# Placing the block sums of a channel MLP, and moving two column copies from VectorE to GpSimd

## The chip, the cores and the metric

The kernel runs on one core of a Trainium2 chip. The metric is the device time of one execution in microseconds (us), from the launch to the end on that core. Three executions of the kernel before took 618.13, 616.25 and 618.18 us; their median is 618.13 us. Inputs and the output are float32 in HBM; inside the chip the operands of the matrix products are fp16 and their sums are float32 in PSUM.

## What is computed

The input is x with 8 batches of 3008 positions and 256 features. First the real part of a two-dimensional Fourier transform over positions and features is taken, and then an MLP mixer block is applied to it: a token MLP across the positions and a channel MLP across the features, each with a residual add.

```python
X = np.fft.fft(np.fft.fft(x, axis=1), axis=2).real           # (8, 3008, 256)
h = np.maximum(X.transpose(0, 2, 1) @ w_tok1, 0) @ w_tok2     # 3008 -> 256 -> 3008
u = X + h.transpose(0, 2, 1)
h2 = np.maximum(u @ w_ch1, 0) @ w_ch2                         # 256 -> 1536 -> 256
return (u + h2).astype(np.float32)
```

## The kernel before

**Stages.** For each batch b, a generator `front(b)` (lines 436 to 567) makes the transform and the token MLP and yields after each small piece: products in PSUM tiles `pz`, `pw`, `pt1`, `pq`, `py`, `pu`, with a VectorE (DVE) or ScalarE (ACT) instruction behind each. Its result is u, laid out with features on the partitions, in six tiles `ut` of 512 positions (the last has 448). Another generator, `fold(b)` (line 414), prepares the input of a batch with fp16 adds on DVE, from SBUF to SBUF. The channel MLP takes one `ut` tile at a time. There are 6 tiles in each of 8 batches, so 48 blocks.

**The two halves of a block.** `mm1` (line 584) makes the hidden layer: 12 groups of 128 hidden features, each two TensorE (PE) products of 128x512 and a ReLU on ACT into the tile `c1` (called c in the profile). `mm2` (line 673) makes the output from `c1`, adds the residual u, and stores it. 42 of the 48 blocks use `mm2_sums` (line 620), a two-by-two block scheme that needs seven block products in place of eight; the other six are called `plain` (line 581) and multiply directly. The scheme needs sums of quarters of `c1`, which DVE makes in `block_sums` (line 599). Four instructions are made for the lower three groups of each half of `c1` (`slice(0, 3)`, called "lower" below) and four for the upper three (`slice(3, HC)`, "upper"):

- number 0: sb0 = a21 + a22
- number 1: sb1 = sb0 - a11
- number 2: a21 = a11 - a21, written over a21 in `c1`
- number 3: sb2 = a12 - sb1

**The order of work.** It is written out by hand; each engine takes its instructions in program order. A block has four steps s = 0 to 3, and `sub = 4 * c + s` counts the 24 steps of a batch. In each step PE gets three of the 12 groups of `mm1` for the current block, then `mm2` step s for the block before (`prev`), with pieces of the front work around it: `own` are the last pieces of this batch's front, `nxt` those of the next batch's, half of them before `mm2` and half after. `plan` and `own_plan` say how many pieces each step takes, and `fold` pieces come at the end of a step from sub 10 (15 in the first batch). In this text "step 1" means s = 1.

**What each step of mm2_sums reads.** Step 0: `c1` directly. Step 1: sb0, then sb1. Step 2: the new a21. Step 3: a22, then sb2. The PSUM tiles are px and py (`pa` and `pb` in the code). The second product of step 1 goes to the part of px that the first product of step 0 used, and waits until DVE has read px in step 0 (line 645, `osb<-px,m` in the profile). The DVE reads in step 3 are `osb<-px,rt` and `osb<-py,m`.

**The residual.** `turn_u` (line 571) transposes `ut` by DMA from SyncE's queue into `rt`, four buffers in turn. `edges` (line 611) copies one or two columns within `rt` (two instructions for c of 3 to 5, otherwise one; 72 in all), so that one slice can be read backwards. A part of the residual is added on GpSimd (POOL): 128x256 float32 in step 0 (line 646) and 128x512 in step 3 (line 660), SBUF to SBUF, 42 of each. POOL's queue also issues the loads of x (`load_x`, line 122).

**Where the sums stand.** In the kernel before: upper 0 and 1 in step 0 behind `mm1`; upper 2 and 3 in step 1 behind `mm1`; lower 0 and 1 in step 2 behind `mm2`; lower 2 and 3 in step 3 behind `mm2`.

Of the kernel before, what the change touches and what calls it, by code (L numbers as in the profile page):

```python
# [40 lines left out]
def kernel(  # L41
# [9 lines left out]
    nc = tc.nc  # L51
# [70 lines left out]
    def load_x(b, between=(None, None)):  # L122
        xp = xin.tile([KR, NR, D], FP16, tag="xp", name="xp")
        xm = xin.tile([KG, NR - 1, D], FP16, tag="xm", name="xm")
        for i in range(2):
            for q, n in ((0, 32), (32, NQ - 32)):
                p0 = i * NQ + q
                nc.gpsimd.dma_start(
                    out=xp[p0:p0 + n, :, :],
                    in_=dram(x_t, (b * S + 16 * i + 64 * q) * D,  # L130
                             [[64 * D, n], [1, NR * D]]))
        xmf = xm[:].rearrange("p t d -> p (t d)")
        for k in range(2):
            if between[k] is not None:
                between[k]()
            gather(xmf[:, 8 * D * k:8 * D * (k + 1)], x8, ix8[0:KG, b, k:k + 1])
        return xp, xm
# [23 lines left out]
    for t in (tp, tq):  # L161
        for i in range(2):
            h = slice(64 * i, 64 * i + 64)
            nc.scalar.activation(
                out=t[h, :, 64 - 64 * i:128 - 64 * i],
                in_=pcol[h, :].unsqueeze(2).to_broadcast([64, NG, 64]),
                func=AFT.Copy, scale=0.0)
    nc.scalar.activation(out=w1m[64:128, NG - 1, :],
                         in_=pcol[64:128, :].to_broadcast([64, DTOK]),
# [52 lines left out]
    HC = NCT // 2  # L222
    wst = const.tile([P, 4, HC, P], FP16, tag="wst")

    def weight_sums():
        b11, b12, b21, b22 = (wc2[:, HC * j:HC * j + HC, P * k:P * k + P]
                              for j in range(2) for k in range(2))
        for o, x, y, op in ((0, b12, b11, AT.subtract), (2, b22, b12, AT.subtract),
                            (1, wst[:, 2], b11, AT.add), (3, b21, wst[:, 1], AT.subtract)):
            nc.vector.tensor_tensor(out=wst[:, o], in0=x, in1=y, op=op)  # L230

    def swap_wc1(h):
        nc.sync.dma_start(out=wc1[1][:, h, :], in_=wc1[0][:, h, :])
        nc.sync.dma_start(out=wc1[1][0:1, h, :], in_=wc1[0][0:1, 1 - h, :])
# [172 lines left out]
    def align_w2(j):  # L407
        th, k = j // 4, slice(16 * (j % 4), 16 * (j % 4) + 16)
        copy(0, w2p[:, th, k, 0:NQ], w2v[:, th, k, :])
# [4 lines left out]
    def fold(b, engs):  # L414
        xp, xm = x_tiles.pop(b)
        eo = perb.tile([KR, NR, D], FP16, tag="eo", name="eo")
        state[b] = {"eo": eo}
        add, sub = AT.add, AT.subtract
        for s, (t0, t1) in enumerate(((13, 17), (9, 13), (5, 9), (1, 5))):
            tt = engs[s].tensor_tensor  # L420
            t = slice(t0, t1)
            rv = slice(16 - t0, 16 - t1 if t1 < 17 else None, -1)
            tt(out=xp[:, t, 1:D], in0=xp[:, t, 1:D], in1=xm[0:KR, rv, D - 1:0:-1], op=add)
            yield
            if t0 == 1:
                tt(out=xp[:, 1:NR, 0], in0=xp[:, 1:NR, 0], in1=xm[0:KR, ::-1, 0], op=add)
                tt(out=eo[:, :, 0], in0=xp[:, :, 0], in1=xp[:, :, 0], op=add)
                t = slice(0, t1)
            tt(out=eo[:, t, 1:129], in0=xp[:, t, 1:129], in1=xp[:, t, 255:127:-1], op=add)
            yield  # L430
            tt(out=eo[:, t, 129:256], in0=xp[:, t, 1:128], in1=xp[:, t, 255:128:-1],
               op=sub)
            yield
# [137 lines left out]
    def turn_u(b, c):  # L571

        rt = work.tile([P, 4, D + 16], FP16, tag="rt", name="rt", bufs=4)
        for h in range(2):
            nc.sync.dma_start_transpose(
                out=rt[:, :, h * P:(h + 1) * P], in_=state[b]["ut"][c][:, h, :])
        return rt
# [3 lines left out]
    def plain(b, c):  # L581
        return (b, c) == (0, 0) or c + 1 == NCH and (b % 2 == 0 or b + 1 == BB)

    def mm1(b, c, c1, cts):
        ut = state[b]["ut"][c]
        n = min(CW, S - CW * c)
        wc = wc1[c >= 3]
        for i in cts:
            ct = CTS[i]
            pc = ps_mm("pc")  # L590
            for h in range(2):
                nc.tensor.matmul(pc[:, 0:n], lhsT=wc[:, h, ct * P:(ct + 1) * P],  # L592
                                 rhs=ut[:, h, 0:n], start=(h == 0), stop=(h == 1))
            if i % 3 < 2 or (b, c) != (0, 0):
                nc.scalar.activation(out=c1[:, ct, 0:n], in_=pc[:, 0:n], func=AFT.Relu)  # L595
            else:
                ts(c1[:, ct, 0:n], pc[:, 0:n], 0.0, AT.max)

    def block_sums(c1, sb, k, which):
        hi = slice(HC + k.start, HC + k.stop)  # L600
        a11, a21 = c1[:, k, 0:D], c1[:, k, D:CW]
        a12, a22 = c1[:, hi, 0:D], c1[:, hi, D:CW]
        sums = ((sb[:, 0, k], a21, a22, AT.add),
                (sb[:, 1, k], sb[:, 0, k], a11, AT.subtract),
                (a21, a11, a21, AT.subtract),
                (sb[:, 2, k], a12, sb[:, 1, k], AT.subtract))
        for i in which:
            o, x, y, op = sums[i]
            nc.vector.tensor_tensor(out=o, in0=x, in1=y, op=op)  # L609

    def edges(rt, c):
        for o, i in ((D, 0), (0, P)) if c >= 3 else ((D, P),):
            nc.vector.tensor_copy(out=rt[:, :, o:o + 1], in_=rt[:, :, i:i + 1])

    lower, upper, turned_ = slice(0, P), slice(P, D), slice(D, P, -1)

# [100 lines left out]
    def pair(b, c1):  # L717

        if b % 2 == 0 and b + 1 < BB:
            state["ch"] = work.tile([P, NCT, 64], FP16, tag="ch", name="ch")  # L720
            nc.vector.tensor_copy(out=state["ch"][:], in_=c1[:, :, CW - 128:CW - 64])
        elif b % 2:
            nc.vector.tensor_copy(out=c1[:, :, CW - 64:CW], in_=state["ch"][:])


    def take(g, n):
        for _ in range(n):
            next(g, None)
# [41 lines left out]
    prev = None  # L770
    turned_u = {(0, 0): turn_u(0, 0)}
    for b in range(BB):
        nxt = front(b + 1) if b + 1 < BB else iter(())
        folds = fold(b + 2, [nc.vector] * 4) if b + 2 < BB else None
        for c in range(NCH):
            c1 = work.tile([P, NCT, CW], FP16, tag="c1", name="c1", bufs=2)
            box = {"rt": turned_u.pop((b, c))}
            if not plain(b, c):
                box["sb"] = work.tile([P, 3, HC, D], FP16, tag="sb", name="sb", bufs=2)
            if c + 1 == NCH and b % 2:  # L780
                pair(b, c1)
            for s in range(4):
                sub = 4 * c + s
                n = plan[b > 0][sub]
                mm1(b, c, c1, range(3 * s, 3 * s + 3))
                if s < 2 and prev is not None and not plain(*prev[0:2]):
                    block_sums(prev[2], pbox["sb"], slice(3, HC), (2 * s, 2 * s + 1))
                take(own, own_plan[b > 0][sub])
                take(nxt, n // 2)
                if prev is not None:  # L790
                    mm2(*prev, s, pbox)
                if s >= 2 and not plain(b, c):
                    block_sums(c1, box["sb"], slice(0, 3), (2 * s - 4, 2 * s - 3))
                if b == 0 and sub < 16 and sub % 2:
                    align_w2(sub // 2)
                take(nxt, n - n // 2)
                if s == 2 and c + 1 < NCH:
                    turned_u[b, c + 1] = turn_u(b, c + 1)
                if s == 3 and c + 1 == NCH and b + 1 < BB:
                    turned_u[b + 1, 0] = turn_u(b + 1, 0)  # L800
                if b == 0 and sub == 4:
                    weight_sums()
                if b == 0 and sub == 3:
                    for h in range(2):
                        swap_wc1(h)
                if b == 0 and 3 <= sub < 9:
                    take(early, 2)
                    if sub == 8:
                        x_tiles[2] = load_x(2)
                if folds is not None and sub >= fold_at[b > 0]:  # L810
                    take(folds, 1 + (b == 0))
                    if sub == fold_at[b > 0] + (5 if b == 0 else 11) and b + 3 < BB:
                        x_tiles[b + 3] = load_x(b + 3)
            if c + 1 == NCH and b % 2 == 0:
                pair(b, c1)
            prev, pbox = (b, c, c1), box
        own = nxt
# [32 lines left out]
```

## Time and profile before

| what | value |
|---|---|
| median of the three executions | 618.13 us |
| the profiled execution, own time | 616.26 us |
| its span, first to last instruction | 614.2 us |
| outside the span (the difference) | 2.1 us |
| granted TensorE clock | 1.000 |
| ACT busy | 442.0 us (72%) |
| POOL busy | 139.3 us (23%) |
| `edges` on DVE (L613) | 72 instructions, 13.3 us, mean 184 ns |
| POOL add in step 0, 128x256 | 42, mean 758 ns |
| POOL add in step 3, 128x512 | 42, mean 1437 ns |

The profile is of one execution, and every duration in this text is from it. A group line gives the line of the kernel, engine and operation, output and inputs by the program's names, shapes and a count, then the busy time of the group in us, the mean of one instruction in ns, and the idle time of the engine just before them. A row of the timeline gives the start and the length in us; rows of one kind that follow one another are merged ("x24"), and in brackets stands the idle time before the row and what ended it. PE products overlap in these records, so the row of a later product can begin before the row of an earlier one ends.

### The profile page before, as it was taken

The numbers are of one execution on the slowest core, as the hardware profiler recorded it, in microseconds if no ns is written. First come the engines' busy times: TensorE is split into PE (matmuls) and PEld (weight loads), VectorE is DVE, ScalarE is ACT, GpSimd is POOL, SyncE is SP. The second block draws the span as 40 slices with busy tenths as digits, with TensorE's granted clock in tenths as the row PEclk, the third lists the DMA queues.
The fourth block names the chain that finished last, engine by engine and source line by source line (L and its number), as shares of the span: only waits on it lengthen the run. The fifth ranks groups of instructions, "written<-read, shape, count | busy, mean of one in ns | idle before, by whom it ended". The sixth has DMA issues, their size and how long they took to land.

```text
span 614.2 us, 15694 instructions
## 1 busy us (share of the span) xinstructions
PE 589.1 (96%) x6322; PEld 422.5 (69%) x6322; DVE 492.8 (80%) x1086; ACT 442.0 (72%) x996; POOL 139.3 (23%) x163
## 2 busy tenths in 40 slices
PE   2899999999999999999999999999999999999996
PEld 1766767667776767767676777766776767766675
DVE  8768879668998699768988789857899778867684
ACT  8866986677767777686766767777777777667772
POOL 8500413111142121302114221311121212101121
PEclk9999999999999999999999999999999999999999
DMA  8994842725347323672419234392222433232433
GB/s 137 210 192 93 183 67 56 162 57 84 53 89 141 85 52 68 118 120 52 97 44 174 53 83 74 61 183 61 53 62 58 91 53 75 65 69 60 88 62 94
DMA packets 86600, 56.52 MB, mean 92 GB/s; under 512 B 54864, under 2 KB 83472, under 8 KB 85776
## 3 DMA queue, kind: packets, MB, share of 16 engines
q1 hardware_dynamic: 78048, 37.84, 30.9%
q0 software_dynamic: 8256, 17.49, 16.5%
q8 instruction: 49, 0.80, 0.5%
q10 hardware_dynamic: 224, 0.20, 0.1%
q14 instruction: 23, 0.19, 0.1%
HBM read 34.98 MB, written 24.64 MB: 97 GB/s over the span
## 4 chain that ended last, share of the span: by engine, by line
PE 80%; DVE 8%; ACT 6%; issue 3%; POOL 1%; DMA 1%; DVEq 0%; POOLq 0%
PE pc L592 33%; PE px L633 20%; PE py L633 7%; PE pu L552 6%; PE po L690 4%; PE pt L488 3%; ACT c L595 3%; DVE sb L609 2%; DVE osb L618 2%; PE pz L445 1%; PE pw L472 1%; PE pw L473 1%; DVE ut L560 1%; PE py L519 1%; DVE yt L526 1%
## 5 line engine op out<-in xcount | busy, mean ns | idle before, releaser
L595 ACT ACTIVATE c<-pc 128x512 f16<-128x512 f32 (+1 forms) x572 | 295.8, 594 | 39.2 <-PE pc L592 19.8
L618 POOL TENSOR_TENSOR osb<-osb,rt 128x256 f32<-128x256 f32 x84 | 92.2, 1097 | 438.5 <-DVE osb L618 411.4
L592 PE MATMUL pc<-ut,wc1p 128*128 128x512 f16 x576 | 140.3, 379 | 0.0
L592 PE MATMUL pc<-ut,wc1m 128*128 128x512 f16 (+1 forms) x576 | 134.9, 370 | 0.0
L633 PEld LDWEIGHTS <-c 128*128 128x128 f16 x2016 | 121.3, 98 | 19.4 <-issue 0.3
L633 PEld LDWEIGHTS <-sb 128*128 128x128 f16 x1512 | 90.2, 98 | 14.1 <-issue 5.0
L638 ACT ACTIVATE m<-px 128x256 f32<-128x256 f32 x126 | 48.6, 386 | 69.9 <-PE px L633 45.2
L592 PEld LDWEIGHTS <-wc1p 128*128 128x128 f16 x576 | 52.2, 98 | 49.0 <-issue 2.3
L560 DVE TENSOR_TENSOR ut<-pu,yt 128x512 f16<-128x512 f32 (+1 forms) x96 | 64.1, 669 | 26.1 <-PE pu L552 26.1
L592 PEld LDWEIGHTS <-wc1m 128*128 128x128 f16 x576 | 53.0, 98 | 46.3
L609 DVE TENSOR_TENSOR sb<-c,sb 128x768 f16<-128x768 f16 x84 | 84.4, 1004 | 0.0
L633 PE MATMUL px<-wst,c 128*128 128x128 f16 x1008 | 70.0, 219 | 0.0
L633 PE MATMUL px<-wc,c 128*128 128x128 f16 x1008 | 63.1, 219 | 0.0
L618 DVE TENSOR_TENSOR osb<-py,m 128x256 f32<-128x256 f32 x84 | 35.4, 422 | 29.4 <-ACT m L638 23.2
L290 ACT ACTIVATE z<-pz 128x480 f16<-128x480 f32 (+1 forms) x60 | 40.1, 672 | 19.4 <-PE pz L445 12.4
L552 PE MATMUL pu<-w2p,uu 128*128 128x512 f16 (+1 forms) x168 | 50.0, 379 | 0.0
L609 DVE TENSOR_TENSOR c<-c 128x768 f16<-128x768 f16 x84 | 49.5, 590 | 0.0
L609 DVE TENSOR_TENSOR sb<-sb,c 128x768 f16<-128x768 f16 x84 | 46.9, 558 | 2.9
L609 DVE TENSOR_TENSOR sb<-c 128x768 f16<-128x768 f16 x84 | 45.9, 547 | 2.4 <-ACT c L595 2.4
L475 DVE SCALAR_TENSOR_TENSOR w<-alt,pw 128x131 f16<-128x131 f16 x96 | 33.0, 350 | 14.4 <-ACT w L290 14.3
L633 PE MATMUL px<-wst,sb 128*128 128x128 f16 x504 | 34.9, 219 | 3.2 <-DVE osb L618 2.6
L526 DVE TENSOR_TENSOR yt<-py,qs 128x512 f16<-128x512 f32 x48 | 30.8, 683 | 8.8 <-ACT qs L522 8.8
(163 smaller groups left out, 674.3 us busy)
## 6 DMA issues: line engine op xcount, KB each, us to landing
out_dram<-osb SPq DMA_DIRECT2D x83, 256.0 KB, 3.7
xp<-in_x_dram POOLq DMA_DIRECT2D x16, 272.0 KB
out_dram<-osb SPq DMA_DIRECT2D x11, 192.0 KB, 3.2
xp<-in_x_dram POOLq DMA_DIRECT2D x16, 127.5 KB
rt<-ut SPq DMA_TRANSPOSE x96, 3.4
w2s<-in_moe_w_tok_dram POOLq DMA_DIRECT2D x1, 1504.0 KB
w1p<-in_moe_w_tok_dram POOLq DMA_DIRECT2D x2, 384.0 KB
wc<-in_moe_w_ch_dram POOLq DMA_DIRECT2D x1, 768.0 KB
```

The source lines that it names most:

```text
L290: nc.scalar.activation(out=out_, in_=in_, func=AFT.Copy)
L475: nc.vector.scalar_tensor_tensor(out=w[:, g, 0:131], in0=alt[:], scalar=pw[:, 131:132], in1=pw[:, 0:131], op0=AT.mult, op1=AT.add)
L526: nc.vector.tensor_tensor(out=yt[:, h, CW * c:CW * c + CW], in0=py[:], in1=qs[:], op=op)
L552: nc.tensor.matmul(pu[:, 0:n], lhsT=uu[:, th, int(minus), h, :], rhs=w2_cols(b, c)[:, th], start=(th == 0), stop=(th == 1))
L560: nc.vector.tensor_tensor(out=ut[:, h, 0:n].rearrange("p (a b) -> p a b", b=64), in0=pu[:, 0:n].rearrange("p (b a) -> p a b", b=64), in1=y ...
L592: nc.tensor.matmul(pc[:, 0:n], lhsT=wc[:, h, ct * P:(ct + 1) * P], rhs=ut[:, h, 0:n], start=(h == 0), stop=(h == 1))
L595: nc.scalar.activation(out=c1[:, ct, 0:n], in_=pc[:, 0:n], func=AFT.Relu)
L609: nc.vector.tensor_tensor(out=o, in0=x, in1=y, op=op)
L618: eng.tensor_tensor(out=o, in0=x, in1=y, op=AT.add)
L633: nc.tensor.matmul(o[:, t], lhsT=a(k)[:, f:f + P], rhs=w(k), start=(first and t == 0 and k == 0), stop=(k == HC - 1), skip_group_check=True)
L638: nc.scalar.activation(out=m[:, i], in_=pa[:, 0], func=AFT.Copy)
L690: nc.tensor.matmul(po[0:n, o:o + D], lhsT=c1[:, ct, ks * P:ks * P + n], rhs=wc2[:, ct, :], start=(ct == 0), stop=(ct == NCT - 1))
```

## The change

Two edits. `edges` issues its copies on GpSimd in place of DVE. And three of the four places of `block_sums` change: upper 0 and 1 go behind the first front pieces of step 0, just ahead of `mm2`; upper 2 and 3 go to the end of step 1, behind `mm2` and all front pieces of the step; lower 2 and 3 go in front of everything in step 3 but `mm1`. Lower 0 and 1 stay where they were. Nothing is computed that was not computed before, and the instructions of PE, ACT and SyncE keep their order.

```diff
     def edges(rt, c):
         for o, i in ((D, 0), (0, P)) if c >= 3 else ((D, P),):
-            nc.vector.tensor_copy(out=rt[:, :, o:o + 1], in_=rt[:, :, i:i + 1])
+            nc.gpsimd.tensor_copy(out=rt[:, :, o:o + 1], in_=rt[:, :, i:i + 1])
...
                 mm1(b, c, c1, range(3 * s, 3 * s + 3))
-                if s < 2 and prev is not None and not plain(*prev[0:2]):
-                    block_sums(prev[2], pbox["sb"], slice(3, HC), (2 * s, 2 * s + 1))
+                def now():
+                    which = 2 * (s % 2), 2 * (s % 2) + 1
+                    if s >= 2 and not plain(b, c):
+                        block_sums(c1, box["sb"], slice(0, 3), which)
+                    elif s < 2 and prev is not None and not plain(*prev[0:2]):
+                        block_sums(prev[2], pbox["sb"], slice(3, HC), which)
+
+                if s == 3:
+                    now()
                 take(own, own_plan[b > 0][sub])
                 take(nxt, n // 2)
+                if s == 0:
+                    now()
                 if prev is not None:
                     mm2(*prev, s, pbox)
-                if s >= 2 and not plain(b, c):
-                    block_sums(c1, box["sb"], slice(0, 3), (2 * s - 4, 2 * s - 3))
+                if s == 2:
+                    now()
                 if b == 0 and sub < 16 and sub % 2:
                     align_w2(sub // 2)
                 take(nxt, n - n // 2)
+                if s == 1:
+                    now()
```

## The prediction

> **What bounds the kernel now.** I read the page first (engine totals and the DVE groups), then the waits, then the timeline of two places where TensorE is late.
>
> ```profile
> PE 589.1 (96%) x6322; PEld 422.5 (69%) x6322; DVE 492.8 (80%) x1086; ACT 442.0 (72%) x996; POOL 139.3 (23%) x163
> L609 DVE TENSOR_TENSOR sb<-c,sb 128x768 f16<-128x768 f16 x84 | 84.4, 1004 | 0.0
> L609 DVE TENSOR_TENSOR c<-c 128x768 f16<-128x768 f16 x84 | 49.5, 590 | 0.0
> L609 DVE TENSOR_TENSOR sb<-c 128x768 f16<-128x768 f16 x84 | 45.9, 547 | 2.4 <-ACT c L595 2.4
> ```
>
> The four sums have one shape; sum 3 (`sb<-c,sb`) costs 1004 ns where sum 0 costs 547. But PE carries the time, so what matters is where PE waits:
>
> ```profile
> PE px L633 <- DVE osb L618: 2.6, 8, 0.8
> PE pz L445 <- DVE ut L560: 1.6, 3, 0.7
> ```
>
> These understate the waits, since product records overlap. The chain of waits has 24 of the px products in 1.34 us, so 12 take 0.67. Counting from start to start in this way over the whole trace I get, after 40 us, 11.5 us of PE waits: 5.6 at the second product of step 1 (15 places, waiting for `osb<-px,m`), 2.1 at `pz`, 1.9 at the token products (1.3 of it in the first batch), the rest small. That is the most that any order of DVE can give back.
>
> Place A, which recurs in five batches:
>
> ```profile
> 300.06 0.42 DVE L618 TENSOR_TENSOR osb<-py,m 128x256 f32<-128x256 f32 x1
> ...
> 300.40 0.55 DVE L609 TENSOR_TENSOR c<-c 128x768 f16<-128x768 f16 x1
> 300.56 1.41 POOL L618 TENSOR_TENSOR osb<-osb,rt 128x512 f32<-128x512 f32 x1 [5.92 <-DVE osb L618]
> ...
> 300.87 1.52 DVE L609 TENSOR_TENSOR sb<-c,sb 128x768 f16<-128x768 f16 x1
> ...
> 302.58 0.41 DVE L431 TENSOR_TENSOR eo<-xp 94x508 f16<-94x508 f16 x1
> ...
> 304.13 0.83 PE L633 MATMUL py<-wst,sb 128*128 128x128 f16 x12
> 304.23 0.38 DVE L613 COPY rt<-rt 128x4 f16<-128x4 f16 x2
> 304.61 0.42 DVE L618 TENSOR_TENSOR osb<-px,m 128x256 f32<-128x256 f32 x1
> ...
> 305.09 0.83 PE L633 MATMUL px<-wst,sb 128*128 128x128 f16 x12
> ```
>
> Sum 3 starts inside POOL's add and ends 0.42 us after it (301.97, 302.39): it stood still. px could start at 304.13 + 0.67 = 304.80 and starts at 305.09, so 0.29 us are lost.
>
> Place C, at three of the changes of batch:
>
> ```profile
> 326.14 0.41 DVE L618 TENSOR_TENSOR osb<-px,rt 128x256 f32<-128x256 f32 x1
> 326.47 0.41 DVE L618 TENSOR_TENSOR osb<-py,m 128x256 f32<-128x256 f32 x1
> ...
> 327.28 2.04 DVE L609 TENSOR_TENSOR sb<-c,sb 128x768 f16<-128x768 f16 x1
> ...
> 327.72 1.18 POOL L618 TENSOR_TENSOR osb<-osb,rt 128x512 f32<-128x512 f32 x1
> 327.76 1.50 PE L633 MATMUL px<-wc,c 128*128 128x128 f16 x24
> ...
> 329.25 0.68 DVE L560 TENSOR_TENSOR ut<-pu,yt 128x512 f16<-128x512 f32 x1
> ...
> 329.98 0.37 PE L445 MATMUL pz<-t1n,eo 94*128 94x96 f16 x5 [0.72 <-DVE ut L560]
> ```
>
> The blocked sum makes L560 late, and pz waits for its PSUM buffer: 327.76 + 1.34 = 329.10, so 0.88 us. Later in the same block px (332.95) waits a further 0.37.
>
> **What the Trainium skill says.** "SBUF — State Buffer", section "SBUF: two separate sides": GpSimd shares a port pair with those DVE instructions that read two SBUF inputs or run in a two-port mode; it is an exclusive lock for a whole instruction, and the loser blocks. The trace agrees: 52 of the 84 sums 3 overlap a POOL add, and these average 1287 ns against 546 for those that don't; L475, with a PSUM input, takes 351 in both cases. "Perfetto Trace Analysis", "Identifying the Most-Contended Engine", warns that matmul busy share misjudges headroom; hence my count from starts. "GPSIMD Engine Reference", "Performance pitfalls for Q7 kernels", gives about 2.9 cycles an element for reads with steps over 8 bytes: for 4 elements next to nothing, so the fixed cost of a POOL instruction decides.
>
> **The change part by part.** I replay the measured rows in the new order, PE's natural times kept, ends overlapping by 0.08 us as in the trace. DVE loses 52 x (1287 - 546) = 38.5 us of standing in sum 3 and 13.3 us of edges; part of the standing comes back wherever the next SBUF instruction follows POOL's add.
>
> 1. *Lower 2 and 3, now ahead of the reads in step 3.* The reads come up to 0.95 us later where DVE is busy. Cover: the next px product has 1.2 to 3.0 us in hand behind `osb<-px,rt` in the stretches with fold work, and keeps at least 0.25. Cost 0; without cover up to 0.3 us a block.
>    - C: `osb<-px,rt` ends at 327.49, before PE needs it at 327.76; `osb<-py,m` at 327.83; L560, which reads PSUM, runs beside POOL's add, 327.75 to 328.43; pz waits no more. L526 waits for ACT (328.76), upper sums to 331.15, `osb<-px,m` to 331.49, before px's natural 332.95 - 0.37 - 0.88 = 331.70. Gain 1.25, 1.25 and 0.72 us at the three changes (the third pz wait is 0.35): **-3.2**.
>    - A: POOL's add moves to 301.5 to 302.9. What collides now is the fold L431, which ends at about 303.35; L475; upper 0 and 1 from 303.54 to 304.68; `osb<-px,m` ends at 305.02. Before: 305.03. Nothing gained, the collision has changed its victim.
> 2. *Upper 0 and 1 behind the first pieces of step 0.* In the blocks before the odd changes of batch (such as 174.87, waiting 0.37) L526, held by ACT until 171.89, now stands ahead of them, and `osb<-px,m` ends at 174.62 in place of 174.82: gain 0.2. Three such, two even ones with 0.1, and half of an unexplained 0.35 us of DVE standing at 318.5: **-1.0**. The last summed block, with no front work (px at 599.26, waiting 0.36): the copy L723 collides in place of sum 3, and edges are gone, so `osb<-px,m` ends 0.3 earlier: **-0.3**. Blocks such as 293.48, with 0.47 us in hand, lose: there before, POOL had waited for `c<-c` and sum 3 slipped through; now L429 collides until 292.40, then a tail copy and L560 come ahead of the sums, and `osb<-px,m` ends at 294.45, px wanted 294.36: 0.14 each in five blocks.
> 3. *Upper 2 and 3 at the end of step 1.* They now stand behind that step's last piece. At 284.62 L475 waits for ACT; the new a21 would be ready at 285.45, while px (285.25) wants its fourth weight at about 285.36: 0.14 with the release, in six blocks: **+0.7**. In A the same gives 0.08, in five blocks: **+0.4**. Queued behind are sum 3, the fold piece and `osb<-py,m`, all with room.
> 4. *Edges on POOL.* Behind them in POOL's queue are the step-0 adds and x loads, in front the step-3 add; nothing there is late (POOL is 23% busy). The plain blocks' DVE reads wait for them, more than a step later. Their price on POOL is not shown: the nearest rows are 128x1 operations of 92 (memset) to 636 ns; I take 0.2 each. On DVE they free 0.17 or 0.38 us in step 0, counted above. But POOL runs them as soon as its step-3 add ends, just where DVE's sums stand, so each can hold DVE once: between 0 and 0.4 us. I take half of it where DVE is late: 0.12 in five A and five D blocks: **+1.2**, with D's 0.14 x 5: **+0.7**.
> 5. *First batch.* The replay from 80 to 98 us moves a 0.99 us wait by -0.26 and adds about 0.5 at the new a21; the 1.28 us wait at 97.39 stays within 0.1, as DVE is the limit until there. **0 +- 1**.
>
> Sum: -3.2 - 1.0 - 0.3 + 0.7 + 0.4 + 1.2 + 0.7 = **-1.5 us**. Against the profiled execution 616.26 that is 614.8; the median of the three runs is 1.87 above that execution, and on it the forecast is 618.13 - 1.5 = 616.6.
>
> **The rivals.**
> - *Much of the wait goes* (R1). If edges cost DVE nothing and folds collide less than replayed, A, D and the first batch gain too: 4.5 + 1.5 (A) + 1 (first batch) - 0.7 = 6.3, so 611.8. For it: 52 us of DVE time leave. Against: in A and D the same POOL add meets the next fold.
> - *The collision only moves* (R2). C's gain is eaten by edges at the full 0.4 us in A and D (+2.8 more than taken): 618.1 to 619.5. For it: A.
> - *The new a21 is late* (R3), slower. Place: px in step 2. Price: sums 2 and 3 lost a step of lead, and have about 0.1 us in hand where a piece ends step 1 (subs 9, 17, 21). Point: once DVE is more than 0.1 us later than replayed, each microsecond goes to PE. At 0.4 us in three places of each of seven batches it is +8.4 - 1.1 (counted) = +7.3, net +5.8; at half of that about +2: 620 to 624. For it: L475 ends step 1 behind an ACT wait. Against: at 21 the replay had the sum ready 0.06 us early.
> - *It doesn't do what it says:* edges on POOL bring new POOL work to the sums it moved; that is part of R2.
>
> **How the numbers follow.** Forecast (gain of 0 to 3.5) 0.43; R1 (over 3.5) 0.17; R2 0.20; R3 0.20. Three runs of this kernel can't tell less than 0.3%, 1.85 us. Of the forecast 0.18 lies beyond a gain of 1.85, so faster 0.35, same 0.25 + 0.20 = 0.45, slower 0.20. The likeliest alone: 614.6 to 618.2. The range takes in R2, the nearer half of R1 and the start of R3: 612.5 to 620.3.
>
> **What would show it.** L609 `sb<-c,sb` near 550 to 600 ns; fold rows L423, L429, L431 longer by up to 0.7 us on average; no pz wait at the changes of batch; px waits of step 1 still there in A, and new ones in step 2 behind `c<-c`. I am wrong if px of step 2 waits in most blocks, or if POOL's copies take 0.4 us or more, or if A's wait is gone.

## The result, and the profile after

Four executions of the changed kernel took 610.33 to 612.49 us, median 612.1; four of the kernel before on the same chip took 616.25 to 618.18, median 617.82. The ratio is 0.9907, with a 95% interval of 0.988 to 0.9933. So the change saves 5.7 us, where the prediction had 1.5. The profiled execution took 611.73 us and its span is 610.0, in place of 616.26 and 614.2.

From the page of the changed kernel, the engine totals and the groups of the four sums (last columns: busy us, mean ns of one, idle us before):

```profile
PE 589.6 (97%) x6322; PEld 423.1 (69%) x6322; DVE 454.9 (75%) x1014; ACT 442.3 (73%) x996; POOL 148.9 (24%) x235
L609 DVE TENSOR_TENSOR sb<-sb,c 128x768 f16<-128x768 f16 x84 | 50.3, 598 | 2.9
...
L609 DVE TENSOR_TENSOR sb<-c 128x768 f16<-128x768 f16 x84 | 48.5, 577 | 2.3 <-ACT c L595 2.3
...
L609 DVE TENSOR_TENSOR sb<-c,sb 128x768 f16<-128x768 f16 x84 | 47.1, 561 | 0.0
...
L609 DVE TENSOR_TENSOR c<-c 128x768 f16<-128x768 f16 x84 | 46.5, 554 | 0.0
```

Sum 3 went from 1004 to 561 ns, 37.3 us in all; sums 0 and 1 took over 6.0 us of it (45.9 and 46.9 us before). DVE lost 37.9 us of busy time (492.8 to 454.9); PE's hardly moved (589.1 to 589.6). As a page of busy times that tells little: 37.9 us left DVE, and 5.7 left the kernel. The waits of PE in the same trace (total us, times, longest):

```profile
PE pt L488 <- DVE w L475: 0.7, 1, 0.7
...
PE px L633 <- DVE osb L618: 0.2, 1, 0.2
PE px L633 <- DVE c L609: 0.2, 1, 0.2
```

Before, this view had `px <- osb` 2.6 us in 8 places and `pz <- ut` 1.6 in 3. The second is gone, the first is down to one entry, and a small wait for `c` is new: that is the new a21 in step 2. Since this view understates waits, I counted them again from start to start of PE's instructions, now from the first product of `mm1` on (38.4 us into the span) and with waits of 0.1 us included, which the prediction's 11.5 us left out for the greater part:

| PE's waits, us (places) | before | after |
|---|---|---|
| px, second product of step 1 | 5.56 (15) | 1.32 (7) |
| pz at the changes of batch | 2.69 (9) | 0.57 (6) |
| token products, for L475 | 1.94 | 1.65 |
| px in step 2, for the new a21 | none | 0.86 (7) |
| all | 13.83 | 8.16 |

The parts not listed are 3.6 us before and 3.8 after, in many waits of about 0.1 us. Where the count cuts off moves both sums alike: with waits above 0.06 us only, they are 11.49 and 5.79. The fall, 5.67 us, agrees with that of the median, 5.7. The two spans differ by less, 4.2 us, because in this profiled execution the work ahead of the first `mm1` product, which the change doesn't touch, ended at 39.81 us in place of 38.43; profiles of other kernels below fall at 38.4 or at 39.6 to 39.8 as well.

### The profile page after: what moved, and what is told of

It reads as the page before. It is cut to its first block, busy times and chain, and to the rows that moved or that the text cites. A ratio compares the mean times of both kernels' runs of the same rounds, so it can differ in the third digit from the quotient of the medians.

```text
span 610.0 us, 15700 instructions
## 1 busy us (share of the span) xinstructions
PE 589.6 (97%) x6322; PEld 423.1 (69%) x6322; DVE 454.9 (75%) x1014; ACT 442.3 (73%) x996; POOL 148.9 (24%) x235
## 4 chain that ended last, share of the span: by engine, by line
PE 92%; DVE 4%; ACT 3%; issue 1%; DVEq 0%; POOL 0%; POOLq 0%
PE pc L592 39%; PE px L633 23%; PE py L633 9%; PE pu L552 7%; PE po L690 4%; PE pt L488 3%; PE pz L445 2%; PE pq L519 1%; PE py L519 1%; PE pw L472 1%; PE pw L473 1%; DVE sb L609 1%; PE filler L283 1%; DVE w L475 1%; DVE xp L423 0%
## 5 line engine op out<-in xcount | busy, mean ns | idle before, releaser
L618 POOL TENSOR_TENSOR osb<-osb,rt 128x256 f32<-128x256 f32 x84 | 79.6, 948 | 381.7 <-DVE osb L618 364.9
L560 DVE TENSOR_TENSOR ut<-pu,yt 128x512 f16<-128x512 f32 (+1 forms) x96 | 64.6, 674 | 51.2 <-PE pu L552 51.1
L609 DVE TENSOR_TENSOR sb<-sb,c 128x768 f16<-128x768 f16 x84 | 50.3, 598 | 2.9
L609 DVE TENSOR_TENSOR sb<-c 128x768 f16<-128x768 f16 x84 | 48.5, 577 | 2.3 <-ACT c L595 2.3
L475 DVE SCALAR_TENSOR_TENSOR w<-alt,pw 128x131 f16<-128x131 f16 x96 | 33.0, 350 | 21.5 <-ACT w L290 21.0
L609 DVE TENSOR_TENSOR sb<-c,sb 128x768 f16<-128x768 f16 x84 | 47.1, 561 | 0.0
L609 DVE TENSOR_TENSOR c<-c 128x768 f16<-128x768 f16 x84 | 46.5, 554 | 0.0
L633 PE MATMUL py<-wst,sb 128*128 128x128 f16 x504 | 35.2, 219 | 0.1
```

Source lines behind the costliest of these rows:

```text
L475: nc.vector.scalar_tensor_tensor(out=w[:, g, 0:131], in0=alt[:], scalar=pw[:, 131:132], in1=pw[:, 0:131], op0=AT.mult, op1=AT.add)
L560: nc.vector.tensor_tensor(out=ut[:, h, 0:n].rearrange("p (a b) -> p a b", b=64), in0=pu[:, 0:n].rearrange("p (b a) -> p a b", b=64), in1=y ...
L618: eng.tensor_tensor(out=o, in0=x, in1=y, op=AT.add)
L633: nc.tensor.matmul(o[:, t], lhsT=a(k)[:, f:f + P], rhs=w(k), start=(first and t == 0 and k == 0), stop=(k == HC - 1), skip_group_check=True)
```

## The experiments

Two theories. *PORT*: the time came from moving the sums away from POOL's add, as the change's shape suggests. *EDGES*: it came from taking the copies of L613 off DVE, because they stood directly ahead of the read `osb<-px,m` that PE waits for. Every run was timed beside the kernel before, whose median was 617.56 in the session of the first three experiments and of the last, and 617.59 in that of the others (on another chip).

| kernel | median us | lowest | ratio, 95% interval | PE's waits in the loop |
|---|---|---|---|---|
| before | 617.6 | 616.25 | 1 | 13.83 |
| after | 612.1 | 610.33 | 0.9907 [0.988, 0.9933] | 8.16 |
| edges alone | 611.9 | 611.25 | 0.9918 [0.99, 0.9936] | 9.06 |
| sums alone | 615.33 | 615.27 | 0.9977 [0.9968, 0.9987] | 12.76 |
| lower 2 and 3 alone | 612.48 | 612.42 | 0.9933 [0.9915, 0.9952] | 10.02 |
| no POOL add in step 3 | 608.38 | 608.38 | 0.9863 [0.9843, 0.9882] | 6.22 |
| no copies at all | 611.39 | 611.35 | 0.9911 [0.9894, 0.9928] | 8.89 |
| edges and lower 2 and 3 | 609.28 | 609.25 | 0.9881 [0.9864, 0.9899] | 7.07 |
| after, upper 2 and 3 unmoved | 610.98 | 609.77 | 0.9893 [0.9876, 0.9909] | 7.59 |
| after, upper 2 and 3 a little earlier | 610.98 | 609.63 | 0.9888 [0.987, 0.9905] | 7.68 |

The last column serves to tell neighbours apart, as the medians contain the set-up. What a kernel gains by its lowest time (from the 616.25 of before) and what it gains in this column agree within 0.5 us in every row.

**Edges alone, and sums alone.** The first makes only the first edit, the second only the other.

```diff
-            nc.vector.tensor_copy(out=rt[:, :, o:o + 1], in_=rt[:, :, i:i + 1])
+            nc.gpsimd.tensor_copy(out=rt[:, :, o:o + 1], in_=rt[:, :, i:i + 1])
```

> Edges on POOL alone, the sums where they were. Theory PORT (the gain of the change is the end of sum 3's standing behind POOL's step-3 add, and edges matter little): sum 3 stays near 1000 ns, both pz waits of 0.88 us and the token waits stay, and POOL's copies hold the upper sums about as long as the edges took on DVE: 0 to -1 us. Theory EDGES (the two copies stand directly ahead of the read that px waits for, and POOL's copies cost DVE nothing): the wait of the second product of step 1 falls by up to 0.38 us in each of its 15 places, from 5.6 to about 1.2 us: -4 to -4.6 us, most of the gain of the change.

> The sums moved as in the change, edges left on DVE. PORT: nearly the whole gain of the change, -4 to -5 us, sum 3 near 560 ns, no pz wait. EDGES: the pz waits go (-2.1), but the px waits of step 1 come back, since behind the change px had only 0.15 to 0.43 us in hand where two copies take 0.38 us on DVE: about 0.53 in six places, 0.2 in three to six; new waits of 0.1 for the new a21; in all -1.5 to -2.5 us.

The copies alone take 4.8 us of waits away, and 5.7 off the median; the sums alone take 1.1 and 2.2, though they take 26.4 us of busy time off DVE (492.8 to 466.4). EDGES had it: for the copies by more than it said, for the sums with less than its 1.5 to 2.5 by the count. The waits of PE with edges alone:

```profile
PE pz L445 <- DVE ut L560: 1.6, 3, 0.7
...
PE px L633 <- DVE osb L618: 0.5, 1, 0.5
```

`pz` waits as before, `px` once, in the first batch: 15 places with 5.56 us have become one with 0.68. And this without any relief for the sums. Source L609 in the kernel before, with edges alone, and with the POOL add left out (shortest, median and longest ns of the 84):

```profile
L609 DVE TENSOR_TENSOR sb<-c,sb x84: 541/1025/2046, 59.4 to 599.6; 128x768 f16<-128x768 f16 x84
```

```profile
L609 DVE TENSOR_TENSOR sb<-c,sb x84: 542/1026/2042, 59.4 to 594.8; 128x768 f16<-128x768 f16 x84
```

```profile
L609 DVE TENSOR_TENSOR sb<-c,sb x84: 541/550/1031, 59.4 to 591.4; 128x768 f16<-128x768 f16 x84
```

With edges alone more than half of the sums 3 still stand behind POOL, and it costs PE nothing at px. Place A, timeline of that kernel:

```profile
298.99 1.34 POOL L618 TENSOR_TENSOR osb<-osb,rt 128x512 f32<-128x512 f32 x1 [6.06 <-DVE osb L618]
...
299.23 1.52 DVE L609 TENSOR_TENSOR sb<-c,sb 128x768 f16<-128x768 f16 x1
...
300.28 0.79 POOL L613 COPY rt<-rt 128x4 f16<-128x4 f16 x2
...
302.49 0.83 PE L633 MATMUL py<-wst,sb 128*128 128x128 f16 x12
302.59 0.42 DVE L618 TENSOR_TENSOR osb<-px,m 128x256 f32<-128x256 f32 x1
...
303.16 0.33 PE L633 MATMUL px<-wst,sb 128*128 128x128 f16 x3
```

Sum 3 takes 1.52 us, as before the change, and the collision is the same. But `osb<-px,m` is ready at 303.01, the px product starts at 303.16 = 302.49 + 0.67, and there is no wait. The read ends 0.15 us before px is wanted. In the kernel before, two copies of 0.38 us together stood directly ahead of this read, it ended 0.23 late, and the wait was 0.29. On POOL the copies ran at 300.28, right behind the add.

**Only lower 2 and 3 to the front of step 3.** The one move of sums that the prediction credited with its largest gain, copies still on DVE.

```diff
+                if s == 3 and not plain(b, c):
+                    block_sums(c1, box["sb"], slice(0, 3), (2, 3))
...
-                if s >= 2 and not plain(b, c):
+                if s == 2 and not plain(b, c):
                     block_sums(c1, box["sb"], slice(0, 3), (2 * s - 4, 2 * s - 3))
```

> Only lower sums 2 and 3 go to the front of step 3; upper sums and edges as in the kernel before. PORT: most of the gain, -3 to -4.5 us, with sum 3 near 600 ns; the pz waits of 2.1 us go. If instead the collision only changes its victim (fold, or upper sum 0, which now follow POOL's add at once): the pz waits go, the px waits stay as they are within 1 us: about -2 us, and sb<-c (sum 0) grows from 547 to 700 to 1000 ns.

Waits 10.02, so 3.8 less, the same as between the lowest times. All of `pz`'s avoidable wait is gone (2.69 to 0.57), and of px's 5.56 us in 15 places 3.74 in 10 remain: the five at A are still 0.28, and those at C are 0.44, 0.44 and 0.34. Most of the sums 3 are freed, from source L609 of this kernel:

```profile
L609 DVE TENSOR_TENSOR sb<-c x84: 537/548/1519, 55.0 to 592.4; 128x768 f16<-128x768 f16 x84
L609 DVE TENSOR_TENSOR sb<-c,sb x84: 542/549/1028, 57.6 to 595.6; 128x768 f16<-128x768 f16 x84
```

The median of sum 3 is 549 ns and its mean 633. But part of the collisions has moved to sums 0 and 1, whose means rise from 547 and 558 to 663 and 689 ns (the longest sum 0 takes 1519): this much of the expectation's second case is true. So this single move is worth 3.8 us alone, yet all three moves together are worth 1.1: the two moves of upper sums give back 2.7 us while the copies are on DVE (px waits 6.13 in place of 3.74, and 0.81 at the new a21). PORT got this move's size right and the whole wrong.

**Edges and lower 2 and 3.** The two edits above together; upper sums where they were before.

> Edges on POOL and lower sums 2 and 3 at the front of step 3; both upper moves undone. If the two gains are of different waits (edges: px of step 1; lower: pz) and the upper moves only cost: product waits in the loop of about 6.5 to 7 us in place of 13.8 before and 8.2 with the whole change, so -7 us, about 1.3 us faster than the whole change. If the upper moves are needed once the lower sums have moved (to keep sum 0 away from POOL's add): px waits of about 2 to 3 us stay, and it is no faster than the whole change.

Waits 7.07, median 609.28. `pz <- ut` is gone and px waits once:

```profile
PE pt L488 <- DVE w L475: 1.0, 2, 0.7
PE pu L552 <- ACT qs L522: 0.7, 1, 0.7
PE px L633 <- DVE osb L618: 0.5, 1, 0.5
```

This is the fastest complete kernel of the study, 1.1 us ahead of the change both in waits and in the lowest time; the medians differ by 2.8, but their intervals against before overlap. Its sums are slower than those of the change, by the groups of the page by form:

```profile
L609 DVE TENSOR_TENSOR sb<-sb,c 128x768 f16<-128x768 f16 x84 | 57.9, 689 | 2.9
L609 DVE TENSOR_TENSOR sb<-c 128x768 f16<-128x768 f16 x84 | 55.7, 663 | 2.3 <-ACT c L595 2.3
...
L609 DVE TENSOR_TENSOR c<-c 128x768 f16<-128x768 f16 x84 | 49.7, 592 | 0.0
```

689, 663 and 592 ns against 598, 577 and 554: more standing on DVE, less waiting on PE.

**The two moves of upper sums.** First the whole change but with upper 2 and 3 left behind `mm1` of step 1 (shown is what differs in the order of work; the run's kernel writes the other places out in full); then the whole change with upper 2 and 3 directly behind `mm2` of step 1, ahead of that step's last front pieces.

```diff
+                if s == 1 and prev is not None and not plain(*prev[0:2]):
+                    block_sums(prev[2], pbox["sb"], slice(3, HC), (2 * s, 2 * s + 1))
...
-                if s == 1:
-                    now()
```

> The whole change except that upper sums 2 and 3 stay behind the hidden layer of step 1. If their move costs what the trace of the whole change shows at the new a21 (0.86 us in 7 places) and gives nothing: those waits go and the time is 0.5 to 1 us below the whole change. If their move had also freed px in step 1: px waits rise and nothing is gained.

```diff
-                if s == 2:
+                if s in (1, 2):
                     now()
...
-                if s == 1:
-                    now()
```

> The whole change, with upper sums 2 and 3 behind the second product of step 1 but ahead of its last front piece. The waits at the new a21 (0.86 us) go as the sums no longer stand behind a front piece that waits for ACT; the front piece is 1 us later, which PE sees only through the token products (0.1 to 0.3 us more). -0.5 to -0.9 us against the whole change; if the token or pz waits take it back, 0.

In the first the wait at the new a21 is gone, in the second one of 0.07 us is left, and the waits are 7.59 and 7.68. So of the change's 8.16, upper 2 and 3 at the end of step 1 cost 0.5 to 0.6 us, and upper 0 and 1 behind the first pieces 7.59 - 7.07 = 0.5 us: six px waits of 0.15 that are not there without this move, less 0.26 at the px wait of the first batch. These differences are below what the medians resolve (both 610.98); they rest on the count in the traces.

**What the copies cost where they are now.** Edges alone, with the copies left out; the upper part of the residual is then read one column off, so its values are those of neighbouring columns.

```diff
     def edges(rt, c):
-        for o, i in ((D, 0), (0, P)) if c >= 3 else ((D, P),):
-            nc.gpsimd.tensor_copy(out=rt[:, :, o:o + 1], in_=rt[:, :, i:i + 1])
+        return
...
-    lower, upper, turned_ = slice(0, P), slice(P, D), slice(D, P, -1)
+    lower, upper, turned_ = slice(0, P), slice(P, D), slice(D - 1, P - 1, -1)
```

> The kernel before with no edges on any engine; the reversed slice is read one column off, so some columns of the residual are wrong. It prices POOL's copies for DVE. If they cost DVE nothing: the same time and the same px waits as with edges on POOL alone, within 0.5 us. If POOL's copies hold the upper sums by their own length: 1.5 to 3 us faster than edges on POOL alone, whose px waits are 0.7 us, so that it would have to come from other waits.

A ratio of 0.9911 against 0.9918, with intervals that all but coincide, and waits of 8.89 against 9.06: on POOL the copies cost PE at most 0.2 us in all. It is mostly they that stand. Source L613 (shortest, median, longest ns) and the groups of POOL by form, of edges alone and then of the change:

```profile
L613 POOL COPY rt<-rt x72: 201/528/1000, 46.6 to 601.5; 128x4 f16<-128x4 f16 x72
L613 POOL COPY rt<-rt 128x4 f16<-128x4 f16 x72 | 30.6, 426 | 43.4 <-DMA rt<-ut 41.9
```

```profile
L613 POOL COPY rt<-rt x72: 197/203/1125, 47.5 to 602.0; 128x4 f16<-128x4 f16 x72
L618 POOL TENSOR_TENSOR osb<-osb,rt 128x512 f32<-128x512 f32 x42 | 51.1, 1217 | 270.1 <-DVE osb L618 260.2 <-DVE ut L544 7.0 <-DVE ut L546 2.8
L613 POOL COPY rt<-rt 128x4 f16<-128x4 f16 x72 | 24.0, 334 | 43.3 <-DMA rt<-ut 41.8
```

**Is it the lock at all?** The kernel before without POOL's add of step 3, which leaves out the upper half's residual.

```diff
-            residual(g, osb[:, :, upper], osb[:, :, upper], rt[:, :, turned_])
```

> The kernel before without POOL's step-3 add (42 of 128x512), so the upper half of the summed blocks' output lacks its residual u. If the lock is what holds sum 3: it falls from 1004 to about 547 ns with no other change to DVE, the pz waits and the px waits of step 1 at places A and C go: -5 to -7 us. If sum 3 is slow for another reason (its operands, or the write of sum 2 just before it): it stays above 900 ns and the time stays within 1 us.

Sum 3's median falls from 1025 to 550 ns (the lines are shown above) with nothing else touched, so POOL's add is what holds it. The mean falls to 634 only: 19 of the 84 still overlap other POOL work and take 926 on average, the other 65 take 548. The time falls by 7.9 us (lowest) to 9.2 (median), more than expected. So freeing DVE of every collision with this add, with the copies still in front of `osb<-px,m`, brings 7.9 us, and edges with lower 2 and 3 brings 7.0 (both by the lowest times) while the add stays.

## Why the prediction was off

Two terms failed, both in the blocks A and D: item 4's price for the copies on POOL (1.2 us expected, nothing measured), and in items 1 and 2 the time for which POOL's add was to hold DVE's fold (the add taken at 1.4 us, measured at 1.16). The sum of the prediction by its own places, beside what the count from starts gives:

| place | predicted | measured |
|---|---|---|
| C, pz and px (item 1) | -3.2 | -3.2 |
| A x5 (items 1, 3, 4) | 0 + 0.4 + 0.6 | -1.45 |
| D, the five blocks like 293.48 (items 2, 4) | +0.7 + 0.6 | 0 |
| blocks before the changes of batch (item 2) | -1.0 | -0.7 |
| last summed block (item 2) | -0.3 | -0.4 |
| new a21, six blocks (item 3) | +0.7 | +0.5 |
| first batch (item 5) | 0 +- 1 | -0.5 |
| sum | -1.5 | -5.7 |

Of the 4.2 us between the sums, 2.4 lie at A (1.4 of the fold, 0.6 of the copies, 0.4 of the new a21) and 1.3 at D (0.7 of the fold, 0.6 of the copies).

**Right.** C is as replayed. From the timeline of the changed kernel:

```profile
326.04 0.68 DVE L560 TENSOR_TENSOR ut<-pu,yt 128x512 f16<-128x512 f32 x1
326.06 1.50 PE L633 MATMUL px<-wc,c 128*128 128x128 f16 x24
326.28 1.18 POOL L618 TENSOR_TENSOR osb<-osb,rt 128x512 f32<-128x512 f32 x1
...
327.40 0.38 PE L445 MATMUL pz<-t1n,eo 94*128 94x96 f16 x5
```

L560 reads PSUM, runs through beside POOL's add, and `pz` starts at 327.40 = 326.06 + 1.34, without a wait where there were 0.88 us. The Trainium skill's "SBUF — State Buffer", "SBUF: two separate sides", says that DVE waits only where it has two SBUF inputs or a two-port mode, and this row agrees: it overlaps the add for 0.44 us, and neither is longer than usual (0.68 for L560, 1.16 to 1.18 for the add). Right in size too are the odd blocks before the changes of batch (replayed stall 0.17, measured 0.15), the last block (though there sum 0 stood, for 1.53 us, and not the copy L723), and the new a21 (0.14 expected, 0.09 measured). The even blocks before the changes of batch were to gain 0.1 each; they wait 0.15 where they had waited 0.1, and a sixth block, at 531.42, waits 0.15 that had not waited. The 0.4 us for the new a21 at A did not come: no wait is there. I have not traced why.

**Wrong: item 4, the price of the copies on POOL.** "I take half of it where DVE is late: 0.12 in five A and five D blocks: +1.2." It is zero: px waits in none of these ten blocks. The step assumed that POOL's copy would get the port and DVE's sum stand. The runs show the reverse. Without the copies the time is the same; and of the copies, which take 0.20 us where they meet nothing (as item 4 took), the median is 0.53 with edges alone, so that it is mostly they that stand. In the changed kernel nothing is added to DVE behind the fold either: from the fold's end to the end of `osb<-px,m` the replay without the copies had 1.67 us at A and 2.05 at D, and the rows below have 1.66 and 2.02.

**Wrong: item 1 at A, "nothing gained, the collision has changed its victim".** In three of the five A blocks the collision did change its victim. Timeline of the changed kernel at one of them:

```profile
229.90 1.16 POOL L618 TENSOR_TENSOR osb<-osb,rt 128x512 f32<-128x512 f32 x1 [7.34 <-DVE osb L618]
229.94 1.40 DVE L431 TENSOR_TENSOR eo<-xp 94x508 f16<-94x508 f16 x1
231.00 1.14 POOL L613 COPY rt<-rt 128x4 f16<-128x4 f16 x2
...
231.53 0.54 DVE L609 TENSOR_TENSOR sb<-c 128x768 f16<-128x768 f16 x1
...
232.48 0.83 PE L633 MATMUL py<-wst,sb 128*128 128x128 f16 x12
232.58 0.42 DVE L618 TENSOR_TENSOR osb<-px,m 128x256 f32<-128x256 f32 x1
...
233.15 0.83 PE L633 MATMUL px<-wst,sb 128*128 128x128 f16 x12
```

The fold stands for 1.40 us, and still the read ends at 233.00, 0.15 us before px is wanted, as in all five with edges alone, where it is sum 3 that stands. So moving the collision from sum 3 to the fold gained and lost nothing, and what is gained is the 0.38 us of the copies. The replay had that 0.38 freed, but spent 0.37 of it on the fold, and its read ended 0.22 late (305.02 against 304.80). Most of the 0.37 is the add, which the replay gave 1.4 us (301.5 to 302.9) and which takes 1.16; the rest, 0.13, I have not traced. In the other two blocks the fold ran free:

```profile
300.71 1.48 POOL L618 TENSOR_TENSOR osb<-osb,rt 128x512 f32<-128x512 f32 x1 [6.70 <-DVE osb L618]
300.75 0.41 DVE L431 TENSOR_TENSOR eo<-xp 94x508 f16<-94x508 f16 x1
...
301.59 0.36 DVE L475 SCALAR_TENSOR_TENSOR w<-alt,pw 128x131 f16<-128x131 f16 x1 [0.43 <-ACT w L290]
...
301.87 0.74 DVE L609 TENSOR_TENSOR sb<-c 128x768 f16<-128x768 f16 x1
...
303.11 0.42 DVE L618 TENSOR_TENSOR osb<-px,m 128x256 f32<-128x256 f32 x1
303.29 0.83 PE L633 MATMUL py<-wst,sb 128*128 128x128 f16 x12
...
303.96 0.33 PE L633 MATMUL px<-wst,sb 128*128 128x128 f16 x3
```

Here L431 takes its usual 0.41, and the add stretches to 1.48, where one that meets nothing takes 1.16 to 1.18. DVE is early, waits 0.43 for ACT at L475, sum 0 takes 0.74 in place of 0.55 because it begins before the add ends (302.19), and `osb<-px,m` ends at 303.53, 0.43 ahead of px. Five waits of 0.29 us are gone in all. The prediction had named this as a sign of being wrong ("if A's wait is gone"). Its sign for the folds, longer by up to 0.7 us on average, did not come either: the means of L423, L429 and L431 went from 747, 550 and 532 to 787, 533 and 634 ns.

**Wrong: item 2 at D.** The plan had the fold held by POOL's add and px 0.14 late in each of five blocks, before the copies. Timeline of the changed kernel:

```profile
289.79 1.16 POOL L618 TENSOR_TENSOR osb<-osb,rt 128x512 f32<-128x512 f32 x1 [8.23 <-DVE osb L618]
289.83 1.41 DVE L429 TENSOR_TENSOR eo<-xp 94x512 f16<-94x512 f16 x1
290.89 0.53 POOL L613 COPY rt<-rt 128x4 f16<-128x4 f16 x1
...
291.79 0.54 DVE L609 TENSOR_TENSOR sb<-c 128x768 f16<-128x768 f16 x1
...
292.84 0.42 DVE L618 TENSOR_TENSOR osb<-px,m 128x256 f32<-128x256 f32 x1
292.85 0.83 PE L633 MATMUL py<-wst,sb 128*128 128x128 f16 x12
```

Here the fold is held as I said, L429 for 1.41 us; so it is in three of the five D blocks, and in the other two it runs in 0.42. But it is held by an add of 1.16. I had taken 1.41 for the add, from the row 300.56 at A of the kernel before, and that row, starting in the middle of a 0.55 us sum, contains a wait of POOL for the port. The term that was mis-sized is the add: 0.25 us too long. And `osb<-px,m` ends at 293.26, before px is wanted at 292.85 + 0.67 = 293.52: 0.26 early, where the plan, with 0.12 for the copies, had 0.26 late. The add and the copies account for 0.37 of these 0.52 us, and the 0.05 us between the end of a read and the start of its px, which the 0.14 contains, for 0.05 more; the rest I have not traced.

**Credit in the wrong place.** The gain of 0.7 us in the blocks before the changes of batch stands under item 2, the move of upper 0 and 1. With edges alone the px waits there vanish altogether, and this move brings 0.15 of each back. The same holds for item 1: it earns its 2.1 us at pz, but the px part of C, 1.1 us, goes with the copies alone and stays with lower 2 and 3 alone (0.44, 0.44 and 0.34 in place of 0.37 each). The forecast added parts which share one reserve, the time DVE has in hand at `osb<-px,m`; whichever comes first gets most of it. The rival R1 named the true course ("if edges cost DVE nothing and folds collide less than replayed") at 611.8 us, with A and the first batch as its gains, and it was held for the less likely case because the folds in A and D were to meet POOL's add. In six of the ten blocks they do, and the waits are gone all the same.

**Left open.** Who gets the port when both rows start within 0.05 us was not tried by itself: in six of these ten blocks the add ran and the fold stood, in four the fold ran and the add stretched. Nor was it tried to leave the copies on DVE and put them behind `osb<-px,m`, which would tell their place in the order from the 13.3 us that they take there. And px itself was left as it is: by the code the second product of step 1 writes `pa[:, 0]`, while the DVE read that it waits for is of `pa[:, 1]`; whether the wait goes when these are two tiles was not tried.

## What to carry to other kernels

Ask first what stands directly ahead of the one instruction that the critical engine waits for: one or two copies of 0.19 us there, block after block, were worth 4.8 us of PE's waits, while moving the sums, which freed twice as much DVE time, by itself was worth 1.1. Price moves against the reserve they share, not one by one: a move worth 3.8 us alone added 2.0 to the copies, and the two other moves lost about half a microsecond each. And take an engine's duration for a replay from a row where it meets nobody, since a row can contain its own wait for a port.

## What was not expected of the hardware

- The recorded duration of a POOL instruction contains its wait for the shared port: the 128x512 add takes 1.16 us at 289.79 and 1.48 at 300.71, beside a fold of 0.41.
- The Trainium skill's "SBUF — State Buffer", "SBUF: two separate sides", gives the lock to whichever starts first. The records don't show who that is at a distance of 0.03 to 0.05 us: in all ten blocks A and D POOL's row begins that much before the fold's, and in six of them DVE waits (229.90, 289.79), in four POOL (300.71). A row's start is therefore not the moment in which the port is taken.
- A copy of four fp16 values per partition takes 169 ns on DVE (median in the kernel before) and 203 on POOL (median in the change), where the sums of 768 values take about 550 on DVE. What it costs on POOL is mostly waiting: the mean is 334 ns in the change and 426 with edges alone.
